# Attention, a mixture layer and a routed mixture in one kernel: the decoding of the weight pieces moves up in the scheduler's priority

## The chip, the cores and the metric

One core of a Trainium2 chip. The metric is the device time of one execution in microseconds, as the median of several runs of the same program. Engines: TensorE (PE in the profile, PEld its weight loads), VectorE (DVE), ScalarE (ACT), GpSimd (POOL) and SyncE (SP), which issues nearly all DMAs here.

## The reference

Three layers follow one another on 4 x 576 tokens of 512 numbers:

```python
# attention: 4 batches, 8 heads, 576 tokens, head size 64, block-causal mask (blocks of 64)
scores = where(block_i >= block_j, q @ k.T / 8, -1e9)
x = softmax(scores) @ v                                  # to [2304, 512]
# first mixture: three matrices 512 x 768, element-wise maximum, then 768 x 512
x = maximum(maximum(x @ w1, x @ w2), x @ w3) @ w_out
# second mixture: tokens with x @ w_skip > 0 go to the best of 8 experts (512 -> 1024 -> 512)
out = x.copy()
out[do] = x[do] + gate * (relu(x[do] @ w1[e]) @ w2[e])
```

## The kernel before, in words

The 2304 tokens are cut into 9 chunks of 256 (`CH`). A chunk's attention is cut into half units, one head of one query tile of up to 128 tokens; chunk 0 and chunk 1 have 16 each. A half unit goes through four steps, each one loop pass later than the one ahead: `s_scores` (L252: score matmuls into `sc`, the negated maximum `nm` on VectorE at L268, the exponential `p` on ScalarE at L273), `s_norm` (L279: the sum's reciprocal `r`, L289, and on GpSimd in the first chunks the product `p*r`, L292), `s_trans` (L296: transposes `tp` on TensorE and the copy `pT`) and `s_pv` (L312: the products `pv` for two heads, then `x`, L325 and L326). For each pair of heads, `load` (L191) asks for keys and queries (`kq`), `load_v` for values (`vt`), and `prep` (L214) splits them into two parts each (`kh`, `kl`, `q`).

Matmul operands are kept as a high and a low part, and three products of parts stand for one product. The weights of the first mixture arrive as int64 pairs and have to be decoded before they are split. `wprep(k)` (L145) does this. For k from 0 to 17 it takes one piece of w1, w2 or w3: a DMA of 512 KB into `raw` (L149, a ring of 3), one pass on ScalarE (L138), four on VectorE (L139 to L142, into `dec`, a ring of 6), the high part on ScalarE (L163) and the low part on GpSimd (L164), into the tile `w`. For k from 18 to 23 it takes one piece of w_out in the same way (`rawo`, one buffer; `deco`; `wo_h`, `wo_l`), and then TensorE transposes it (`pswt`, L168), ScalarE copies that (`wt`, L170), and TensorE multiplies it by the routing weights (`psw`, L173), which gives the routing matrix `wp` (L174, L175). The tiles `wo_h` and `wo_l` take the memory of the rings `raw` and `dec`, so no w_out piece can be split before the last w piece has been decoded and split.

The first mixture's work on a chunk is a generator, `moe_steps` (L434): 18 steps `m_h` of 12 matmuls each (`ps_h`, L338; 6 column blocks times w1, w2, w3), in which chunk 0 also calls `wprep` for the w_out pieces from step 16 on; then `m_logits` (`ps_l`, L359), which needs all of `wp`; then `m_y` (`ps_y`, L375) and the routing. All chunks but the last share one pair of tiles for the hidden layer, so chunk 1 cannot write its own before chunk 0's `m_y` has read it.

The main loop (L510 to L541) goes over half units. In each pass it writes down the attention steps, two calls of `wprep` while pieces of w1 to w3 are left (so all 18 are written within nine passes, in chunk 0), and, once chunk 1 has begun, some steps of the mixture. This is not the order of execution. The framework's scheduler takes instructions by priority, which is the place in the program less an offset, and fixes one order for each engine and for SP's DMA issues; every engine then executes in that order. `pri` (L507) gives the four attention steps an offset of 1000; `load`, `load_v`, `prep`, `wprep` and the mixture have none.

After chunk 8's attention the mixture is finished, and the second mixture (`Moe2`, L563) runs in an order written by hand.

Of the kernel before, what the change touches and what calls it, by code (L numbers as in the profile page):

```python
# [48 lines left out]
def kernel(  # L49
# [36 lines left out]
    wr_sb = const.tile([P, ND, NG], F32, name="wr_sb")  # L86

    _moe1_phase(tc, nc, const, small, locals())


def _moe1_phase(tc, nc, const, small, g):
# [10 lines left out]
    with ExitStack() as st_y:  # L102
# [88 lines left out]
        def load(i):  # L191
            if i >= len(groups):
                return
            c, b, qlo, qhi, tiles, hp = groups[i]
            gd = gdat[i]
            gd["raw"] = kvp.tile([P, 4, CH], F32, tag="kq", name="kq", bufs=3)
            if b == 0:
                for r0 in (0, 64):
                    nc.sync.dma_start(out=gd["raw"][r0:r0 + 64, :, 0:qhi - qlo], in_=kq0[hp, 0:64, :, qlo:qhi])
                return  # L200
            nc.sync.dma_start(out=gd["raw"][:, :, 0:qhi - qlo], in_=kqT[b - 1, hp, :, :, qlo:qhi])

        def load_v(i):
            if i >= len(groups):
                return
            c, b, qlo, qhi, tiles, hp = groups[i]
            gd = gdat[i]
            nkt = (qhi + P - 1) // P
            gd["v"] = kvp.tile([P, 5, P], F32, tag="v", name="vt", bufs=2)
            nc.sync.dma_start(  # L210
                out=gd["v"][:, 0:nkt, :],
                in_=v[b, 0:nkt * P, hp * P:(hp + 1) * P].rearrange("(t p) d -> p t d", p=P))
# [66 lines left out]
        def s_norm(k):  # L279
            i, c, hp, q0, nq, nk, col, j, first = hus[k]  # L280
            h = hd[k]
            su = h["su"]
            r = sm.tile([P, 1], F32, tag="r", name="r")
            eng = nc.gpsimd if c < 3 or (c < 0 and k % 2) else nc.vector
            if h["parts"] == 2:
                eng.tensor_scalar(r[:nq], su[:nq, 0:1], su[:nq, 1:2], 1e-9, op0=ALU.add, op1=ALU.add)
            else:
                eng.tensor_scalar(r[:nq], su[:nq, 0:1], 1e-9, None, op0=ALU.add)
            nc.vector.reciprocal(r[:nq], r[:nq])  # L289
            pt = h["p"][:nq, 0:nk]  # L290
            if c < 4 or (c < 0 and k % 2 == 0):
                nc.gpsimd.tensor_tensor(pt, pt, r[:nq, 0:1].to_broadcast([nq, nk]), op=ALU.mult)  # L292
            else:
                nc.vector.tensor_scalar(pt, pt, r[:nq, 0:1], None, op0=ALU.mult)

        def s_trans(k):  # L296
            i, c, hp, q0, nq, nk, col, j, first = hus[k]
            h = hd[k]
            nkt = (nk + P - 1) // P
            pT = pp.tile([P, 5, P], F32, tag="pT", name="pT")  # L300
            h["pT"] = pT
            for t0 in range(0, nkt, 4):
                n = min(4, nkt - t0)
                tp = ps_t.tile([P, 4, P], F32, tag="tp", name="tp")
                for t in range(n):
                    nc.tensor.transpose(tp[:, t, 0:nq], h["p"][:nq, (t0 + t) * P:(t0 + t + 1) * P], ident[:nq, :nq])  # L306
                if (k + t0) % 2 or c < 2:
                    nc.scalar.copy(pT[:, t0:t0 + n, 0:nq], tp[:, 0:n, 0:nq])  # L308
                else:
                    nc.vector.tensor_copy(pT[:, t0:t0 + n, 0:nq], tp[:, 0:n, 0:nq])  # L310
# [186 lines left out]
        wk = 0  # L497
# [9 lines left out]
        def pri(c):  # L507
            return tc.high_priority(1000 if c >= 0 else 0)

        for k in range(n_hu + 3):  # L510
            if k < n_hu:
                i, c, hp, q0, nq, nk, col, j, first = hus[k]
                if first:
                    load(i + 2)
                    load_v(i + 1)
                with pri(c):
                    s_scores(k)
                if first:
                    prep(i + 1)
            if 0 <= k - 1 < n_hu:  # L520
                with pri(hus[k - 1][1]):
                    s_norm(k - 1)
            if 0 <= k - 2 < n_hu:
                with pri(hus[k - 2][1]):
                    s_trans(k - 2)
            if 0 <= k - 3 < n_hu and hus[k - 3][7] == 1:
                with pri(hus[k - 3][1]):
                    s_pv(k - 3)
                if k - 3 + 1 == n_hu or hus[k - 2][1] != hus[k - 3][1]:
                    queue.append(moe_steps(hus[k - 3][1]))  # L530
            for _ in range(2):
                if wk < 18:
                    wprep(wk)
                    wk += 1
            if k == 0:
                constants()
            if k < n_hu and c > 0:
                credit += NM / per_chunk[c] * (0.8 if c == 1 else 1)
                while credit >= 1:
                    credit -= 1  # L540
                    run_moe()  # L541
# [301 lines left out]
```

## Time and profile before

| What | us |
|---|---|
| median of 3 runs | 765.43 |
| lowest and highest | 764.71, 770.18 |
| the profiled execution, own time | 770.52 |
| its span in the trace | 768.7 |

The profile is of one execution, the one of 770.52 us, of which the span covers 768.7. "Busy" is the time in which an engine executes; the idle time ahead of a group of instructions is given with the engine, tile and line that ended it. Matmuls overlap in the pipeline, so a single matmul's duration is longer than the distance to the next. `xN` is a count. Names of tiles are those of the program, with the numbers left out.

### The profile page before, as it was taken

To read this page: it belongs to the slowest core of one execution; us is meant where nothing else is said; L and a number is where in the kernel's file an instruction comes from. 1 tells how busy PE (TensorE), PEld (TensorE's weight loads), DVE (VectorE), ACT (ScalarE), POOL (GpSimd) and SP (SyncE) were. 2 spreads that over 40 slices of the span, in tenths; PEclk is the share of its full clock that TensorE was granted. 3 is DMA by queue.
4 is the path that set the end of the run, shared out by engine and by line. 5 is a ranking of instruction groups with operands and counts; after the bars stand their busy time and mean duration, and the time that the engine had idled before them with its cause. 6 is when DMAs were issued, how large, how long until landed. Compare 5 with 4: busy or idle time off the path is not lost. (4 is left out here: it accounts for less than half of the span.)

```text
span 768.7 us, 13867 instructions
## 1 busy us (share of the span) xinstructions
PE 668.7 (87%) x4774; PEld 569.6 (74%) x4774; DVE 492.7 (64%) x1291; ACT 375.7 (49%) x977; POOL 348.8 (45%) x434
## 2 busy tenths in 40 slices
PE   2667887889999999999999999999999764888775
PEld 1445776667997998988988978988989643666664
DVE  5898998854655765676765557666645404556774
ACT  4575656634544454545544445554436114354561
POOL 4777876753543322321111233211117608567783
PEclk9988999559999999999999999999999985998999
DMA  8963513433122124323102143212017938847730
GB/s 198 210 189 108 156 49 103 126 103 108 44 55 85 45 63 131 87 63 97 40 23 91 32 117 108 76 35 73 19 56 275 328 115 294 295 119 262 259 123 30
DMA packets 84861, 92.02 MB, mean 120 GB/s; under 512 B 11252, under 2 KB 61556, under 8 KB 84768
## 3 DMA queue, kind: packets, MB, share of 16 engines
q1 hardware_dynamic: 81104, 85.42, 36.9%
q0 software_dynamic: 2624, 5.45, 2.2%
q8 instruction: 47, 0.77, 0.4%
q14 instruction: 46, 0.38, 0.1%
q10 hardware_dynamic: 1040, 0.01, 0.1%
HBM read 80.17 MB, written 11.96 MB: 120 GB/s over the span
## 5 line engine op out<-in xcount | busy, mean ns | idle before, releaser
L338 PE MATMUL ps_h<-x,w 128*128 128x256 f32 x1944 | 275.4, 290 | 6.7 <-DVE x L326 2.4
L338 PEld LDWEIGHTS ps_h<-x,w 128*128 128x128 f32 x1944 | 251.5, 193 | 13.1 <-DVE x L326 3.3
L273 ACT ACTIVATE p<-sc,nm 64x288 f32<-64x288 f32 (+9 forms) x192 | 95.5, 500 | 51.2 <-PE tp L306 26.6
L306 PE MATMUL tp<-cst_sb,p 128*128 128x128 f32 (+1 forms) x480 | 90.9, 285 | 13.6 <-ACT pT L308 7.4
L268 DVE TENSOR_REDUCE nm<-sc 64x1 f32<-64x288 f32 (+9 forms) x192 | 84.9, 450 | 27.3 <-PE sc L263 24.1
L261 PE MATMUL sc<-kh,q 128*64 128x288 f32 (+9 forms) x192 | 71.8, 378 | 24.7 <-ACT p L273 14.3
L646 POOL TENSOR_TENSOR lo<-raw,hi 128x1024 fp32r<-128x1024 f32 x30 | 83.7, 2812 | 17.3 <-ACTq L774 9.6
L242 POOL TENSOR_TENSOR kl<-kq,kh 64x512 fp32r<-64x512 f32 (+3 forms) x48 | 52.3, 1089 | 83.3 <-ACT kh L241 82.8
L350 POOL TENSOR_TENSOR h_l<-hm,h_h 128x256 fp32r<-128x256 f32 x54 | 43.9, 814 | 94.5 <-ACT h_h L349 92.0
L306 PEld LDWEIGHTS tp<-cst_sb,p 128*128 128x128 f32 (+1 forms) x480 | 57.3, 147 | 32.4 <-issue 14.0
L323 PE MATMUL pv<-pT,vt 128*64 128x128 f32 (+1 forms) x960 | 75.6, 286 | 5.3 <-ACT pT L308 3.3
L646 DVE TENSOR_TENSOR lo<-raw,hi 128x1024 fp32r<-128x1024 f32 x30 | 66.6, 2231 | 17.1 <-ACT hi L642 14.9
L642 ACT CAST hi<-raw 128x2048 fp32r<-128x2048 f32 x30 | 56.4, 1904 | 29.3 <-PEq L774 17.7
L323 PEld LDWEIGHTS pv<-pT,vt 128*64 128x64 f32 x960 | 52.9, 147 | 22.4 <-issue 7.5
L292 POOL TENSOR_TENSOR p<-p,r 128x128 f32<-128x128 f32 (+8 forms) x72 | 57.4, 801 | 25.2 <-DVE r L289 20.1
L261 PEld LDWEIGHTS sc<-kh,q 128*128 128x128 f32 (+1 forms) x192 | 36.8, 193 | 37.6 <-ACT p L273 20.0
L263 PE MATMUL sc<-kl,q 128*64 128x288 f32 (+9 forms) x192 | 63.6, 336 | 0.5 <-DVE kl L182 0.5
L308 ACT COPY pT<-tp 128x256 f32<-128x256 f32 (+4 forms) x112 | 44.9, 401 | 37.2 <-PE tp L306 32.4
L277 POOL MEMSET p<- 128x64 f32 (+1 forms) x96 | 14.4, 156 | 99.0 <-PE tp L306 89.0
L310 DVE COPY pT<-tp 128x256 f32<-128x256 f32 (+4 forms) x80 | 35.1, 446 | 36.7 <-PE tp L306 36.2
L241 ACT CAST kh<-kq 128x512 fp32r<-128x512 f32 (+3 forms) x48 | 24.5, 511 | 49.1 <-DMA kq<-in_kqT_dram 43.1
L326 DVE TENSOR_TENSOR x<-pv,x 128x128 fp32r<-128x128 f32 (+1 forms) x80 | 21.6, 270 | 37.5 <-ACT x L325 37.3
(137 smaller groups left out, 1162.2 us busy)
## 6 DMA issues: line engine op xcount, KB each, us to landing
raw<-in_m_w_dram SPq DMA_DIRECT2D x32, 1024.0 KB
raw<-in_w_dram SPq DMA_DIRECT2D x18, 512.0 KB
kq<-in_kqT_dram SPq DMA_DIRECT2D x16, 512.0 KB
vt<-in_v_dram SPq DMA_DIRECT2D x16, 320.0 KB
x<-y SPq DMA_DIRECT2D x18, 256.0 KB
out_dram<-y SPq DMA_DIRECT2D x18, 256.0 KB
kq<-in_kq_dram SPq DMA_DIRECT2D x16, 256.0 KB
rawo<-in_w_out_dram SPq DMA_DIRECT2D x6, 512.0 KB
```

Source lines behind the costliest of these rows:

```text
L242: nc.gpsimd.tensor_tensor(kl[0:64, :, qlo:qhi], kraw[0:64], kh[0:64, :, qlo:qhi], op=ALU.subtract)
L261: nc.tensor.matmul(ps[:nq, 0:hi - lo], gd["q1"][:, j, q0:q0 + nq], gd["kh"][:, j, lo:hi], start=True, stop=False)
L263: nc.tensor.matmul(ps[:nq, 0:hi - lo], gd["q2"][:, j, q0:q0 + nq], gd["kl"][:, j, lo:hi], start=False, stop=True)
L268: nc.vector.tensor_reduce(nm[:nq, n:n + 1], pss[n][:nq, 0:hi - lo], axis=AX.X, op=ALU.max, negate=True)
L273: nc.scalar.activation(pt[:nq, lo:hi], pss[n][:nq, 0:hi - lo], AF.Exp, bias=nm[:nq, 0:1], accum_out=su[:nq, n:n + 1])
L292: nc.gpsimd.tensor_tensor(pt, pt, r[:nq, 0:1].to_broadcast([nq, nk]), op=ALU.mult)
L306: nc.tensor.transpose(tp[:, t, 0:nq], h["p"][:nq, (t0 + t) * P:(t0 + t + 1) * P], ident[:nq, :nq])
L308: nc.scalar.copy(pT[:, t0:t0 + n, 0:nq], tp[:, 0:n, 0:nq])
L323: nc.tensor.matmul(pv[64 * jj:64 * jj + 64, 0:nq], vt[:, t, 64 * jj:64 * jj + 64], hd[k - 1 + jj]["pT"][:, t, 0:nq], start=(t == 0), stop= ...
L338: nc.tensor.matmul(ps, a[:, d, :], x[:, d, :], start=(n == 0), stop=(n == 3 * ND - 1))
L642: self.nc.scalar.copy(self.w(e, s)[0], self.raw_of(4 * e + s))
L646: eng.tensor_tensor(lo[:, r], self.raw_of(4 * e + s)[:, r], hi[:, r], op=ALU.subtract)
```

## The change

The two calls of `wprep` in the main loop get the same offset as the attention steps.

```diff
@@ -530,7 +530,8 @@
             for _ in range(2):
                 if wk < 18:
-                    wprep(wk)
+                    with tc.high_priority(1000):
+                        wprep(wk)
                     wk += 1
```

The work is the same: each engine has as many instructions of each line as before (ScalarE has one table load listed at another line). The w_out pieces keep their priority. Lines below L533 have a number higher by one in the changed kernel. Three places show what the scheduler makes of it.

SP at the start, first before, then after. `raw` from in_w1, in_w2 and in_w3 are the first pieces of w1 to w3, `kq` from in_kq0 keys and queries of batch 0, and `vt` values.

```order
L199 DMA kq_120<-in_kq0_dram 64x4x256 x2
L472 DMA aux_sb_117<-in_aux_dram 64x576
L224 DMA auxk_125<-in_aux_dram 64x576
L210 DMA vt_139<-in_v_dram 128x2x128
L475 DMA cst_sb_65<-in_cst_dram 128x282
L199 DMA kq_142<-in_kq0_dram 64x4x256 x2
L210 DMA vt_148<-in_v_dram 128x2x128
L199 DMA kq_145<-in_kq0_dram 64x4x256 x2
L149 DMA raw_118<-in_w1_dram 128x4x256
L149 DMA raw_118<-in_w2_dram 128x4x256
```

```order
L149 DMA raw_118<-in_w1_dram 128x4x256
L149 DMA raw_118<-in_w2_dram 128x4x256
L149 DMA raw_118<-in_w3_dram 128x4x256
L199 DMA kq_120<-in_kq0_dram 64x4x256 x2
L472 DMA aux_sb_117<-in_aux_dram 64x576
L224 DMA auxk_125<-in_aux_dram 64x576
L210 DMA vt_139<-in_v_dram 128x2x128
L475 DMA cst_sb_65<-in_cst_dram 128x282
L199 DMA kq_142<-in_kq0_dram 64x4x256 x2
L149 DMA raw_118<-in_w1_dram 128x4x256
```

The first three w pieces now stand ahead of the first keys and queries, and the fourth ahead of the third pair of heads.

VectorE at the fifth w_out piece (`deco`), in chunk 2's attention, first before, then after; `q` belongs to the second pair of heads of batch 1.

```order
L141 SCALAR_TENSOR_TENSOR deco<-rawo,deco 128x512
L289 RECIPROCAL r<-r 64x1
L270 TENSOR_TENSOR nm<-nm 64x1
L238 COPY q_162<-q_1925 64x2x192
L239 SCALAR_TENSOR_TENSOR q_1925<-kq,q_1925 64x2x192
L326 TENSOR_TENSOR x<-pv,x 128x64
L142 SCALAR_TENSOR_TENSOR deco<-rawo,deco 128x512
L268 TENSOR_REDUCE nm<-sc 64x1
```

```order
L141 SCALAR_TENSOR_TENSOR deco<-rawo,deco 128x512
L174 CAST wp<-psw 128x10
L289 RECIPROCAL r<-r 64x1
L310 COPY pT<-tp 128x4x64
L310 COPY pT<-tp 128x64
L142 SCALAR_TENSOR_TENSOR deco<-rawo,deco 128x512
L175 TENSOR_TENSOR wp<-psw,wp 128x10
L268 TENSOR_REDUCE nm<-sc 64x1 x2
L238 COPY q_162<-q_1925 64x2x192
L239 SCALAR_TENSOR_TENSOR q_1925<-kq,q_1925 64x2x192
```

The piece's last pass (L142) moved ahead of the pair of instructions that prepare `q`.

ScalarE at the sixth w_out piece, from its first pass (L138) to its high part (L163), first before, then after; `kh_124` and `kh_158` are keys of batch 1, each cast once its DMA has landed.

```order
L241 CAST kh_124<-kq 128x2x256
L170 COPY wt<-pswt 128x512
L273 ACTIVATE p,su<-sc,nm 64x64
L138 ACTIVATE deco<-rawo 128x512
L325 CAST x<-pv 128x64
L308 COPY pT<-tp 128x4x64
L241 CAST kh_158<-kq 128x2x256
L308 COPY pT<-tp 128x64
L273 ACTIVATE p,su<-sc,nm 128x192 x2
L163 CAST wo_h<-deco 128x512
```

```order
L138 ACTIVATE deco<-rawo 128x512
L241 CAST kh_124<-kq 128x2x256
L237 ACTIVATE q_2105<-kq 128x2x192
L273 ACTIVATE p,su<-sc,nm 64x64
L163 CAST wo_h<-deco 128x512
L325 CAST x<-pv 128x64
L170 COPY wt<-pswt 128x512
L308 COPY pT<-tp 128x4x64
L308 COPY pT<-tp 128x64
L273 ACTIVATE p,su<-sc,nm 128x192
L241 CAST kh_158<-kq 128x2x256
```

The piece's first pass now stands ahead of the cast of `kh_124`, and its high part and the two copies `pT` ahead of the cast of `kh_158`.

## Rows read from the trace of the kernel before

**Rows 1.** The head of the page, and its line of TensorE's granted clock in 40 equal slices (19.2 us each), in tenths of full speed.

```profile
span 768.7 us, 13867 instructions
...
PEclk9988999559999999999999999999999985998999
```

**Rows 2.** Busy time by stretch from 200 us on. Columns: stretch, its length, then busy us and instructions of PE, PEld, DVE, ACT and POOL, the granted clock, the busy share of the DMA engines, GB/s.

```profile
200.00:300.00 100.00, 100.00 (x801) 89.58 (x802) 61.52 (x202) 48.86 (x154) 35.57 (x67) 1.00 0.23 67
...
500.00:560.00 60.00, 60.00 (x508) 54.82 (x508) 39.63 (x132) 27.07 (x84) 8.72 (x24) 1.00 0.13 41
```

**Rows 3.** The same view of the front of the program, in stretches that end where the text says: the first scores' maximum, the last w piece's decode, the second w_out piece's decode, the first `ps_l`, and TensorE without gaps.

```profile
0.00:14.70 14.70, 2.12 (x6) 1.50 (x6) 6.50 (x14) 4.87 (x9) 5.53 (x11) 1.00 0.79 169
14.70:111.50 96.80, 72.04 (x421) 55.20 (x422) 91.17 (x172) 60.98 (x166) 73.23 (x87) 0.93 0.62 155
111.50:123.70 12.20, 9.08 (x82) 7.29 (x81) 9.17 (x23) 9.04 (x26) 9.26 (x15) 1.00 0.22 60
123.70:155.00 31.30, 24.70 (x174) 19.50 (x174) 27.06 (x67) 19.86 (x62) 22.01 (x31) 0.68 0.42 120
155.00:170.60 15.60, 11.97 (x85) 10.34 (x84) 8.26 (x27) 7.22 (x23) 9.76 (x22) 0.50 0.39 119
170.60:178.00 7.40, 7.40 (x35) 5.47 (x35) 2.19 (x8) 1.88 (x6) 1.15 (x4) 0.64 0.15 38
```

**Rows 4.** VectorE's groups of instructions, shapes apart, from 14.70 to 111.50 us: line, engine, operation, names, shapes, count, busy us, mean ns, idle before it and who ended that.

```profile
L141 DVE SCALAR_TENSOR_TENSOR dec<-raw,dec 128x512 int32<-128x512 int32 x18 | 19.8, 1100 | 0.0
...
L139 DVE TENSOR_SCALAR dec<-dec 128x512 f32<-128x512 f32 x18 | 14.3, 800 | 4.0 <-ACT dec L138 3.9
...
L268 DVE TENSOR_REDUCE nm<-sc 128x1 f32<-128x512 f32 x7 | 4.7, 676 | 0.1
...
L289 DVE RECIPROCAL r<-r 128x1 f32<-128x1 f32 x28 | 4.3, 152 | 0.1
L326 DVE TENSOR_TENSOR x<-pv,x 128x128 fp32r<-128x128 f32 x12 | 3.4, 280 | 0.1
...
L345 DVE TENSOR_TENSOR hm<-ps_h,hm 128x256 f32<-128x256 f32 x4 | 1.6, 410 | 0.0
```

**Rows 5.** The start, in order of time, all engines: start us, duration, engine, line, operation, tiles, count, idle before it and who ended that.

```profile
0.75 1.33 SPq L199 DMA_DIRECT2D kq<-in_kq_dram  x2
...
6.35 1.28 ACT L237 ACT_TABLE_LOAD   x1 [6.35 <-DMA kq<-in_kq_dram]
...
8.30 0.42 DVE L238 CAST q<-q 64x512 fp32r<-64x512 f32 x1 [6.62 <-ACT q L237]
...
11.83 1.15 SPq L149 DMA_DIRECT2D raw<-in_w_dram  x2
...
13.58 0.51 SPq L149 DMA_DIRECT2D raw<-in_w_dram  x1
...
14.70 0.80 DVE L268 TENSOR_REDUCE nm<-sc 128x1 f32<-128x128 f32 x3
...
18.05 0.67 ACT L138 ACTIVATE dec<-raw 128x512 f32<-128x512 f32 x1 [0.74 <-DMA raw<-in_w_dram]
...
23.72 0.67 ACT L138 ACTIVATE dec<-raw 128x512 f32<-128x512 f32 x1 [2.14 <-DMA raw<-in_w_dram]
```

**Rows 6.** The decoded tile `dec`, 0 to 120 us: count, min/median/max ns, first and last start.

```profile
L139 DVE TENSOR_SCALAR dec<-dec x18: 404/548/1483, 19.4 to 105.8; 128x512 f32<-128x512 f32 x18
L140 DVE TENSOR_SCALAR dec<-dec x18: 402/420/1454, 20.9 to 107.5; 128x512 int32<-128x512 int32 x18
L141 DVE SCALAR_TENSOR_TENSOR dec<-raw,dec x18: 666/1016/2193, 21.6 to 108.6; 128x512 int32<-128x512 int32 x18
L142 DVE SCALAR_TENSOR_TENSOR dec<-raw,dec x18: 665/682/1556, 24.8 to 110.8; 128x512 int32<-128x512 int32 x18
```

**Rows 7.** The w_out pieces: SP's DMA issues, then VectorE, then ScalarE, then TensorE, each in order of time.

```profile
155.01 0.47 SPq L160 DMA_DIRECT2D rawo<-in_w_out_dram  x1
...
150.90 0.67 DVE L141 SCALAR_TENSOR_TENSOR deco<-rawo,deco 128x512 int32<-128x512 int32 x1
...
154.30 0.68 DVE L142 SCALAR_TENSOR_TENSOR deco<-rawo,deco 128x512 int32<-128x512 int32 x1
...
162.34 0.69 DVE L142 SCALAR_TENSOR_TENSOR deco<-rawo,deco 128x512 int32<-128x512 int32 x1
...
159.90 0.67 ACT L138 ACTIVATE deco<-rawo 128x512 f32<-128x512 f32 x1
...
163.96 0.62 ACT L241 CAST kh<-kq 128x512 fp32r<-128x512 f32 x1 [3.02 <-DMA kq<-in_kqT_dram]
...
166.01 1.12 PE L168 MATMUL pswt<-cst_sb,deco 128*128 128x128 f32 x4
...
170.60 0.38 PE L359 MATMUL ps_l<-h_h,wp 128*20 128x256 f32 x1
```

**Rows 8.** TensorE at the full clock, chunk 2's attention.

```profile
124.70 0.60 PE L306 MATMUL tp<-cst_sb,p 128*128 128x128 f32 x4
...
128.35 0.29 PE L261 MATMUL sc<-kh,q 128*64 128x288 f32 x1
128.48 0.29 PE L263 MATMUL sc<-kl,q 128*64 128x288 f32 x1
129.23 1.09 PE L323 MATMUL pv<-pT,vt 128*64 128x128 f32 x16 [0.46 <-DVE pT L310]
```

## Prediction

> **What bounds the kernel now.** I read the granted clock by slices first, then busy time by stretch, then VectorE's groups, then the order of time at the two places that the change touches. From 200 us to 560 us TensorE is busy without a gap at the full clock [rows 1, 2]. The two kernels run the same work there, so there the change can gain nothing directly. What it can change is how early TensorE gets there. In the front VectorE is the busy one: from the first maximum of scores (14.70 us) to the end of the last w piece's decoding (111.50 us) it executes 91.17 of 96.80 us, while TensorE executes 72.04; in the next 12.20 us it executes 9.17 [rows 3]. After that no engine is full: from 123.70 to 170.60 us the six w_out pieces follow one another, one at a time through a single raw buffer, and TensorE, partly at 0.50 of its clock, waits among attention's steps for the sixth of them before the first `ps_l` at 170.60 [rows 3, 7]. From there TensorE has no gap [rows 3].
>
> So the time is: when does the first `ps_l` start, and how much of TensorE's work is still to do then. I counted both programs' orders. On TensorE they have executed the same instructions of every kind by the end of the seventh `ps_y` tile (115 score pairs, 262 transposes, 258 `pv`, 864 `ps_h`) and by each later one, so nothing behind that point adds a term.
>
> **The change, part by part.** Nothing is added or removed. Four things move.
>
> *The decoding ends earlier, but the orders meet again.* In the new order VectorE finishes the eighteenth w piece with 26 maxima, 23 reciprocals, 9 evictions of `x` and 4 of the mixture behind it, where it had 30, 28, 12 and 8. At 0.676, 0.152, 0.280 and 0.410 us each [rows 4] that is 2.7 + 0.8 + 0.8 + 1.6 = 5.9 us less work, so the last w piece would be done some 6 us sooner. It buys little: in both orders GpSimd's low part of the second w_out piece stands behind exactly the same work (13 key splits, 32 sums, 33 products, 18 w pieces, 5 of the hidden layer), and VectorE's decoding of it behind nearly the same (35 maxima against 34, 32 reciprocals and 14 evictions in both). What is taken from attention ahead of the last w piece is paid between it and the second w_out piece. Only idle time can differ at that meeting place, which was at 123.70 us.
>
> *The start.* The first `raw` takes the place of the first `kq`: 512 KB each, issued at 0.75; the keys let ScalarE start at 6.35 and VectorE at 8.30 [rows 5]. I take the same for the first piece, so VectorE starts work when it did, with decoding. Three pieces then stand ahead of the first maximum. At the shortest durations that the trace has for the four passes (0.404, 0.402, 0.666 and 0.665 us [rows 6]) they take 3 x 2.14 = 6.4 us, so the first maximum comes at 14.7 + 6.4 = 21.1 us. VectorE was busy in those 6.4 us before and is busy after: cost nothing, as long as VectorE's work is the pace. If that cover is gone, it costs the 6.4 us.
>
> *Idle time up to the meeting place.* Before, VectorE idled 96.80 - 91.17 = 5.63 us in the long stretch, 4.0 of them ahead of L139, waiting for raw data by way of ScalarE [rows 3, 4], and 12.20 - 9.17 = 3.03 us behind it. After, the stretch behind the last w piece holds 5.9 us more of VectorE's work, 15.1 us. At the idle share of that stretch (3.03 in 12.20, a quarter) it idles 5.0 us there, 2.0 more. The stretch ahead is shorter and asks for raw data sooner, for which I give back 1.0 of the 4.0. Sum +1.0. The bounds are -8.7 (all 8.66 us of idle time go) and +6.4 on top of +1.0 (attention's late start is kept whole).
>
> A rule speaks to this. L141 has a least time of 0.666, a median of 1.016 and a most of 2.193 us for one shape [rows 6]. The Trainium skill's SBUF — State Buffer, "Who interferes with whom", says that a VectorE instruction with two SBUF inputs and a GpSimd instruction that reads SBUF exclude each other for their whole length; the spread agrees. By that rule the three first pieces, decoded while GpSimd has little to do, would save 3 x (1.100 - 0.666) = 1.3 us, and the sum below would be 762.4. I leave this out, because the twelve later splits still meet VectorE's passes.
>
> *The fifth and sixth w_out piece.* L141 of the fifth ended at 151.57 and its L142 began at 154.30, behind the `q` pair; at 155.01 SP issued the sixth [rows 7]. In the new order four small instructions stand between; by the distance of such rows about 0.7 us, so 2 us are saved. The sixth piece's L142 ended at 163.03, but its transposes began at 166.01, because the `pv` ahead of them on TensorE waited for a `pT` copy, which waited on ScalarE behind the cast of a key tile whose DMA landed at 163.96 [rows 7]. That cast now stands behind the copies: up to 3.0 us more. Against that, the cast of the other key tile now stands between the piece's first pass and the later copies; I take off 0.5. Together -4.5; bounds 0 (another wait takes over, most likely keys' DMAs) and -5.7 (2.73 + 2.98).
>
> *What is left at the first `ps_l`.* There the new order has executed 53 score pairs, 120 transposes and 110 `pv` instead of 55, 124 and 120. At the full clock the distances are 0.26 us for a pair, 0.15 and 0.068 [rows 8]: 0.5 + 0.6 + 0.7 = +1.8 us, to be done in TensorE's full stretch. This is a count, and sure.
>
> Sum: +1.0 - 4.5 + 1.8 = -1.7 us. The profiled execution took 770.52 us, which would become 768.8. It is 5.1 us over the median of the runs shown; on the median the sum gives 765.43 - 1.7 = 763.7 us.
>
> **The rivals.** A measurement of this kernel can tell about 1% from no change, 7.65 us: faster is below 757.8, slower above 773.1.
>
> *Slower: attention is late and stays late.* Place: the chain from a maximum over exponential, reciprocal, product, transpose, copy and `pv`, in chunk 1, once the decoding no longer fills VectorE. Price: the 6.4 us of the start, the +1.0, no gain at the w_out pieces, since keys and queries then come later too, and the 1.8: +9.2, 774.6 us. It decides from the point at which VectorE idles more than about 15 us up to the meeting place instead of 8.7. For it: VectorE already idled a quarter of the time right after the last w piece [rows 3], and the raw pieces asked for at 11.83 and 13.58 landed at 18.05 and 23.72, so what stands behind others lands 6 to 10 us late [rows 5]. Against it: in the long stretch VectorE had 94% of its time filled, with attention's steps ready. The Trainium skill's DMA: Bandwidth & Descriptors, "Queues, rings and completion order", says that an engine's DMAs use one ring on each DMA engine and are taken up in ring order. By that rule the first keys stand behind 1.57 MB; at the 169 GB/s of the first stretch [rows 3] they land 9.3 us later, at 15.6, and the first maximum would come some 2 us later still, which makes this rival 776.6 us. The landing times in those rows agree with it, and it is why I give this rival more than one in ten.
>
> *Faster: the idle time goes.* With weights ready sooner, TensorE's mixture steps no longer wait and half of the 8.7 us of VectorE's idle time goes, and the w_out pieces gain the whole 5.7: -4.3 - 5.7 + 1.8 = -8.2, 757.2 us. For it: 4.0 us of that idle time are waits for raw data. Against it: a ring of 3 raw tiles still asks for a piece only when the one three before is decoded.
>
> *Faster: the clock.* From 155 us to the first `ps_l` TensorE ran at 0.50 of the full clock, and at 0.64 on the mean until 178.00 [rows 3], after a stretch in which it was busy about four fifths of the time. If the new order keeps it busier there, 11.97 x 0.50 + 7.40 x 0.36 = 8.7 us of its work go: -1.7 - 8.7 = -10.4, 755.0 us. Nothing in the order says that it will be busier, and the opposite would lengthen the spell.
>
> **How the numbers follow.** Forecast, 763.7 us with its own range from 757.9 to 773.0: 0.61. Late attention, 774.6: 0.19. Idle time gone, 757.2: 0.12. Clock, 755.0: 0.08. Hence faster 0.20, within 1% 0.61, slower 0.19. The range goes from 755.0, the clock rival, to 775.0, just past late attention, and leaves out no more than two in ten.
>
> **What would show it.** In the changed kernel's profile: VectorE's first passes are L139 to L142 and begin between 8 and 9 us; the first maximum comes at 20 to 23 us; the last L142 of a w piece ends at 104 to 108 us; the second w_out piece's L142 ends within 3 us of 123.7; the first `ps_l` starts at 165 to 169 us, and TensorE has no gap from there. The forecast is wrong if the second w_out piece is more than 6 us off 123.7 either way, if the sixth piece's transposes still begin behind a key cast on ScalarE, or if a difference arises behind the seventh `ps_y` tile, where the orders are the same.

## The result, and the profile of the changed kernel

The changed kernel is slower: 776.36 us (median of 7 runs) against 768.64 us (7 runs), ratio 1.0122 with a 95% interval of 1.0082 to 1.0161. The forecast was 763.7 us, the range 755.0 to 775.0; the rival that comes nearest is late attention, 774.6 us. A second set of runs of the same two programs gave 1.0103 [1.0047, 1.0160]. Each was profiled twice, and the marks of the two profiles are (us):

| mark | before | changed | mean difference |
|---|---|---|---|
| first maximum (L268) starts | 14.70, 14.58 | 21.89, 21.56 | +7.1 |
| chunk 0's last `x` copy (L325) | 67.57, 65.17 | 82.24, 81.14 | +15.3 |
| L142 of the second w_out piece starts | 122.13, 119.28 | 127.31, 127.53 | +6.7 |
| first `ps_l` | 170.60, 168.09 | 171.86, 171.64 | +2.4 |
| sixth `y` copy (L378) | 300.34, 297.44 | 303.21, 303.59 | +4.5 |
| seventh `y` copy | 347.15, 345.50 | 352.85, 356.75 | +8.5 |
| eighteenth and last `y` copy | 626.96, 623.39 | 631.21, 635.35 | +8.1 |
| end of the span | 768.7, 763.5 | 777.5, 778.7 | +12.0 |

The loss has arisen by the seventh `y` copy. What is added in the second mixture is not settled: from its first gather into `xg` (L654, L655 in the changed kernel) to the end it took 132.7 and 131.1 us before, 137.4 and 134.5 after, but 130.4 in `first3` below, whose ratio is as high as the changed kernel's.

The changed kernel's start, its columns as in [rows 5]: SP, ScalarE, then VectorE.

```profile
0.74 1.53 SPq L149 DMA_DIRECT2D raw<-in_w_dram  x3
2.32 1.39 SPq L199 DMA_DIRECT2D kq<-in_kq_dram  x2
...
0.75 1.28 ACT L138 ACT_TABLE_LOAD   x1 [0.75 <-PEq L831]
4.57 0.66 ACT L138 ACTIVATE dec<-raw 128x512 f32<-128x512 f32 x1 [2.53 <-DMA raw<-in_w_dram]
12.09 0.63 ACT L237 ACTIVATE q<-kq 128x512 fp32r<-128x512 f32 x1 [1.21 <-DMA kq<-in_kq_dram]
...
5.26 0.43 DVE L139 TENSOR_SCALAR dec<-dec 128x512 f32<-128x512 f32 x1 [3.58 <-ACT dec L138]
21.89 0.28 DVE L268 TENSOR_REDUCE nm<-sc 128x1 f32<-128x128 f32 x1
```

The keys were asked for 1.6 us later than in [rows 5], behind three transfers of 0.5 MB, and ScalarE could use them at 12.09 us, 5.7 us after the 6.35 at which it waited no longer for them before. VectorE began at 5.26, earlier than the 8 to 9 of the forecast: ScalarE could use the first piece at 4.57 us, not at 6.35, and its table load, which stood behind the keys' arrival before, was over by then. The Trainium skill's DMA: Bandwidth & Descriptors, "Queues, rings and completion order", from which I had worked out 15.6 us as an estimate, says that each ring is consumed in order; the 12.09 us agree in direction. The rate that I gave it, 169 GB/s, was too low: the DMA engines moved 226 GB/s in the first 12.09 us.

The stretches of [rows 3] in the changed kernel, same columns.

```profile
0.00:14.70 14.70, 0.00 (x0) 0.00 (x0) 7.29 (x12) 6.35 (x12) 4.46 (x11) 1.00 0.94 222
14.70:111.50 96.80, 64.48 (x361) 49.15 (x362) 90.45 (x169) 59.66 (x160) 73.06 (x87) 0.82 0.55 144
111.50:123.70 12.20, 12.20 (x104) 10.76 (x103) 4.84 (x15) 7.34 (x22) 5.96 (x11) 1.00 0.19 54
123.70:155.00 31.30, 25.34 (x181) 19.58 (x179) 23.29 (x62) 19.70 (x60) 20.03 (x28) 0.79 0.39 120
155.00:170.60 15.60, 12.83 (x90) 10.44 (x89) 12.41 (x33) 7.92 (x25) 9.69 (x15) 0.50 0.34 99
```

In the long stretch VectorE is as full as before (90.45 of 96.80 us), but TensorE executes 64.48 us instead of 72.04 (361 matmuls instead of 421), at a mean clock of 0.82 instead of 0.93. In the second profiles it is 363 matmuls instead of 436 with 0.91 in both, so the work is missing without a lower clock too. In the next stretch it is the other way round: TensorE has no gap, and VectorE executes 4.84 us instead of 9.17. I read this as the price of the order, since TensorE's work here comes from attention; the experiments below test it.

Where TensorE's bulk of chunk 0's mixture begins, ScalarE's last `x` copy of chunk 0 and TensorE, in the kernel before:

```profile
67.57 0.28 ACT L325 CAST x<-pv 128x128 fp32r<-128x128 f32 x1
...
71.69 1.70 PE L338 MATMUL ps_h<-x,w 128*128 128x256 f32 x12 [1.09 <-ACT ha L342]
```

and in the changed kernel:

```profile
82.24 0.26 ACT L325 CAST x<-pv 128x128 fp32r<-128x128 f32 x1
...
82.56 1.01 PE L338 MATMUL ps_h<-x,w 128*128 128x256 f32 x3 [0.32 <-ACT x L325]
...
89.54 1.69 PE L338 MATMUL ps_h<-x,w 128*128 128x256 f32 x12
```

Only three `ps_h` tiles can be open at a time, and none is complete before the last of chunk 0's `x`. The matmuls at 82.56 wait for it; the first group of 12 in a row stands at 89.54, 17.9 us later than before. The weights came earlier (the last w piece's L142 starts at 98.89 instead of 110.78), but they were not what came last. This lateness alone is not the price, though: in first1 below the last `x` comes at 75.23 us and the first such group (24 in a row) at 81.23, 9.5 us later than before, and no time is lost.

The end of the w_out pieces, as in [rows 7]:

```profile
127.31 0.69 DVE L142 SCALAR_TENSOR_TENSOR deco<-rawo,deco 128x512 int32<-128x512 int32 x1
...
166.85 1.38 DVE L142 SCALAR_TENSOR_TENSOR deco<-rawo,deco 128x512 int32<-128x512 int32 x1
...
168.28 1.12 PE L168 MATMUL pswt<-cst_sb,deco 128*128 128x128 f32 x4
...
171.86 0.38 PE L359 MATMUL ps_l<-h_h,wp 128*20 128x256 f32 x1
```

The sixth piece's transposes follow its decoding at once, as forecast; before they began 3.0 us behind it [rows 7].

And one gap that the forecast did not have, behind the sixth `y` copy. The changed kernel, in order of time (SP, ScalarE, TensorE):

```profile
307.94 1.79 SPq L201 DMA_DIRECT2D kq<-in_kqT_dram  x2
...
313.99 0.62 ACT L241 CAST kh<-kq 128x512 fp32r<-128x512 f32 x1 [3.33 <-DMA kq<-in_kqT_dram]
...
315.80 0.62 ACT L241 CAST kh<-kq 128x512 fp32r<-128x512 f32 x1 [0.76 <-DMA kq<-in_kqT_dram]
...
316.63 0.26 ACT L308 COPY pT<-tp 128x128 f32<-128x128 f32 x1
...
316.94 1.31 PE L323 MATMUL pv<-pT,vt 128*64 128x128 f32 x20 [2.37 <-ACT pT L308]
```

The same place in the kernel before (SP, ScalarE):

```profile
305.26 0.55 SPq L201 DMA_DIRECT2D kq<-in_kqT_dram  x1
...
309.65 0.62 ACT L241 CAST kh<-kq 128x512 fp32r<-128x512 f32 x1 [2.75 <-DMA kq<-in_kqT_dram]
```

SP asks for two pairs of keys in a row, and both land late; both casts stand on ScalarE ahead of a `pT` copy, and TensorE waits 2.37 us for that. Before, one pair was asked for here; TensorE had no gap in this profile and one of 1.16 us in the second, in which that cast waited 4.44 us. In the second profile of the changed kernel the first cast waited 4.59 us and TensorE 3.5 us, and TensorE's granted clock was 0.50 from 317 to 322 us.

### The profile page after: what moved, and what is told of

It is laid out like the page before. It is cut to its first block, busy times and chain, and to the rows that moved or that the text cites. A ratio compares the mean times of both kernels' runs of the same rounds, so it can differ in the third digit from the quotient of the medians.

```text
span 777.5 us, 13867 instructions
## 1 busy us (share of the span) xinstructions
PE 670.9 (86%) x4774; PEld 571.1 (73%) x4774; DVE 491.7 (63%) x1291; ACT 377.8 (49%) x977; POOL 345.3 (44%) x434
## 5 line engine op out<-in xcount | busy, mean ns | idle before, releaser
L268 DVE TENSOR_REDUCE nm<-sc 64x1 f32<-64x288 f32 (+9 forms) x192 | 85.0, 450 | 40.0 <-PE sc L263 36.8
L306 PE MATMUL tp<-cst_sb,p 128*128 128x128 f32 (+1 forms) x480 | 93.8, 287 | 14.0 <-POOL p L292 8.0
L323 PE MATMUL pv<-pT,vt 128*64 128x128 f32 (+1 forms) x960 | 79.2, 286 | 5.3 <-ACT pT L308 4.0
L647 DVE TENSOR_TENSOR lo<-raw,hi 128x1024 fp32r<-128x1024 f32 x30 | 69.2, 2318 | 15.9 <-ACT hi L643 15.3
L294 DVE TENSOR_SCALAR p<-p,r 128x576 f32<-128x576 f32 (+9 forms) x88 | 41.4, 472 | 4.3
```

The lines of the kernel that those rows point to most:

```text
L268: nc.vector.tensor_reduce(nm[:nq, n:n + 1], pss[n][:nq, 0:hi - lo], axis=AX.X, op=ALU.max, negate=True)
L323: nc.tensor.matmul(pv[64 * jj:64 * jj + 64, 0:nq], vt[:, t, 64 * jj:64 * jj + 64], hd[k - 1 + jj]["pT"][:, t, 0:nq], start=(t == 0), stop= ...
L647: eng.tensor_tensor(lo[:, r], self.raw_of(4 * e + s)[:, r], hi[:, r], op=ALU.subtract)
```

## The experiments

Ratios are to the kernel before on the same chip, with 95% intervals. "Keys" is the start of ScalarE's first pass on the first keys and queries (L237); where the table load waits for the keys (first maximum before 15 us, and late_keys), it lies 1.28 us behind their arrival. "Maxima" is the number of maxima (L268) that VectorE has started when the last pass on the last w piece starts: the fewer, the earlier the decoding stands. "Idle" is TensorE's idle time in the first 181 us of the profile; it depends on the granted clock too, which was 0.77 to 0.89 there. All columns but the ratio are of one profiled execution, and those lie up to 5 us off the median of their kernel.

| kernel | keys | first maximum | maxima | chunk 0's last `x` | idle | ratio |
|---|---|---|---|---|---|---|
| before | 7.64 | 14.70 | 30 | 67.57 | 50.7 | 1 |
| changed | 12.09 | 21.89 | 26 | 82.24 | 55.7 | 1.0122 [1.0082, 1.0161] |
| same_again | 11.72 | 21.56 | 26 | 81.14 | 55.2 | 1.0103 [1.0047, 1.0160] |
| first3 | 10.85 | 20.57 | 27 | 79.25 | 58.8 | 1.0114 [1.0068, 1.0160] |
| late_keys | 12.81 | 19.87 | 30 | 78.72 | 57.6 | 1.0089 [1.0049, 1.0129] |
| gap_prep3only | 10.75 | 20.51 | 26 | 80.94 | 54.7 | 1.0073 [1.0044, 1.0102] |
| raws_pool | 8.71 | 19.13 | 28 | 75.60 | 55.9 | 1.0029 [1.0009, 1.0049] |
| first1 | 7.80 | 15.93 | 27 | 75.23 | 46.9 | 0.9989 [0.9963, 1.0016] |
| from3 | 7.53 | 14.57 | 29 | 78.64 | 55.2 | 1.0034 [0.9998, 1.0071] |
| start_first | 7.55 | 14.60 | 30 | 71.40 | 53.5 | 1.0029 [0.9992, 1.0067] |
| att0 | 7.62 | 14.67 | 29 | 70.01 | 44.9 | 1.0026 [0.9994, 1.0058] |
| b_loads | 7.67 | 14.73 | 29 | 69.89 | 48.6 | 1.0042 [1.0014, 1.0071] |
| b_wokq | 7.53 | 14.58 | 30 | 65.95 | 46.0 | 1.0022 [0.9996, 1.0048] |
| before_light | 7.59 | 14.64 | 34 | 67.76 | 52.4 | 1.0029 [1.0001, 1.0058] |
| after_light | 11.32 | 21.12 | 28 | 81.92 | 63.2 | 1.0109 [1.0075, 1.0142] |
| before_again | 7.53 | 14.58 | 30 | 65.17 | 51.4 | one execution |

The theory after the result was that the late start is the cost; the rivals were the later pieces' place in the order, the transfers' bunching, the gap, and scatter.

**same_again**, the changed kernel once more.

> The changed kernel unaltered, for a second profile of it and more times. In its first profile the last first-mixture output copies stand 4.2 to 5.8 us behind those of the kernel before, and the span 8.8, so some 4.6 us come to the difference inside the second mixture, whose order is the same in both. Theory A (all of the loss that is the change's own arises before the second mixture: late attention, two half units more left over, and a key transfer waited for at 315 us): the 4.6 us are scatter between executions, and the profile of this one has the first gather of the second mixture 4 to 6 us later than before's 636.0, a second mixture within 3 us of before's 132.7 us (first gather to end) or at least other than 137.4. Theory C (the second mixture is slower after the change, by its clock or its transfers): again 137 us or more from the first gather to the end. The ratio to the kernel before is 1.008 to 1.016 under both.

First gather at 644.2 us, 8.2 later than before's, so more than the 4 to 6 expected, and 134.5 us from there to the end. That is theory A's side; theory C's 137 us do not repeat.

**first3** and **from3** take the change apart.

```diff
-                    with tc.high_priority(1000):
+                    with tc.high_priority(1000 if wk < 3 else 0):    # first3
+                    with tc.high_priority(1000 if wk >= 3 else 0):   # from3
```

> Only the first three pieces get the offset, so only SP's start and the engines' heads change: three raw transfers ahead of the first keys, VectorE's decoding ahead of the first maximum. It leaves four tp tiles fewer behind the first ps_l than the changed kernel (57 half units have their tp ahead of it, against 53; before: 55). Theory A1 (the loss comes from the start: the keys behind 1.5 MB of raws, first maximum at 21.9 us instead of 14.7, TensorE short of work up to 80 us): first maximum at 21 to 23 us, first ps_l at 174 to 176 us, later than in the changed kernel since it stands behind four more half units, and the time 771 to 778, ratio 1.006 to 1.014. Theory A2 (the loss comes from the later pieces' place ahead of chunk 1's attention): ratio 0.996 to 1.003.

> The offset for all pieces but the first three: the start is that of the kernel before (keys first, first maximum at 14 to 15 us), and behind it the order is the changed kernel's (53 half units ahead of the first ps_l, as there). Theory A1 (the loss comes from the start): first maximum 14 to 15 us, last w piece's last pass done at 104 to 109 us, first ps_l at 168 to 170 us, and the time within 3 us of the kernel before, ratio 0.996 to 1.004. Theory A2 (the loss comes from the later pieces): ratio 1.008 to 1.016, as the whole change.

The first three pieces alone cost as much as all eighteen. Their first `ps_l` came at 177.5 us, later than the 174 to 176 expected; behind the sixth `y` copy there is no gap (44.9 us to the seventh), so nothing of this loss comes from there. The fifteen others cost 0.3%, not told from nothing. But they hardly moved: 29 maxima stand ahead of the last w piece, 30 before and 26 in the changed kernel, and that piece's last pass began at 110.86 us, where it was to be done at 104 to 109. So from3 says little on the later pieces' place. Its first `ps_l` came at 172.4 us, not at 168 to 170, and the gap behind the sixth `y` copy is there (2.4 us).

**start_first** keeps all eighteen and puts the first loads back in front.

```diff
+        with tc.high_priority(5000):
             load(0)   # ... to load(1), the code ahead of the loop
```

> The change, with the loads and the splitting of the first half units (the code in front of the loop) raised by 5000, so that SP asks for three pairs' keys, values and constants ahead of the first raw transfer; all 18 pieces keep their offset. 56 half units stand ahead of the first ps_l (before 55). Theory A1 (the raws ahead of the first keys cost the time): first maximum at 12 to 15 us and a time of 764 to 771, ratio 0.995 to 1.003. Theory A2 (the pieces' place ahead of the later attention costs it): ratio 1.006 to 1.016.

As the theory has it. But the decoding fell back together with the start: 30 maxima stand ahead of the last w piece, as before, so this run does not part the late start from the early decoding. **first1** and **raws_pool** are doses between.

```diff
+                    with tc.high_priority(1000 if wk < 1 else 0):    # first1
-                nc.sync.dma_start(
+                (nc.gpsimd if k < 3 else nc.sync).dma_start(         # raws_pool, in the changed kernel
```

> Only the first piece gets the offset: one raw transfer of 0.5 MB ahead of the first keys, one piece decoded ahead of the first maximum (three in first3, none in the kernel before). 55 half units stand ahead of the first ps_l, as in the kernel before. Theory A1 (each piece in front of attention delays it by 2.3 to 2.5 us, and TensorE, which is the pace from 90 us on, does not make that up): first maximum at 16.5 to 18 us, first pswt 2 to 3 us behind the 114.2 of before, ratio 1.000 to 1.006, a third of first3's. Theory A3 (a threshold: a start that is late by less than VectorE's slack costs nothing): first pswt within 1 us of 114.2 and ratio 0.996 to 1.001.

> The change, but GpSimd's queue issues the first three raw transfers, so on SP's the first keys, values and constants stand in front again; VectorE's order then has one piece's decoding ahead of the first maximum, and 57 half units are ahead of the first ps_l. Theory Q (the ring's order is the cost: keys behind 1.5 MB): first maximum at 15 to 19 us and a ratio of 0.997 to 1.005. Theory O (the raws cost the keys the same time from whatever queue, since the 16 engines share them): first maximum at 20 to 23 us and ratio 1.007 to 1.015.

One piece ahead costs nothing that can be measured, though the first `pswt` came at 116.6 us instead of 114.2 (A1's mark, A3's ratio). Its keys are usable almost as early as before, while the last w piece stands behind 27 maxima, as in first3, and chunk 0's last `x` comes 7.7 us later than before. So decoding that early, without late keys, lost nothing. In raws_pool SP asks for the keys at 0.74 us and GpSimd for the three raws from 1.31 on; ScalarE takes the keys at 8.71 us, straight behind a decoding pass that had waited for its raw until 8.15. The first maximum comes at 19.13, just outside theory Q's 15 to 19, and most of the loss is gone.

**late_keys** tests the step itself: the kernel before, keys late, nothing decoded earlier.

```diff
+        with tc.high_priority(6000):
+            for i in range(3):
+                nc.sync.dma_start(out=dec_t[:, 2 * i:2 * i + 2]..., in_=ws[i][:, 0:2 * P]...)
         load(0)
```

> The kernel before, without the change, with three extra transfers of 0.5 MB (the first raws, copied a second time into the memory of dec, whose contents nobody reads) ahead of the first keys on SP: attention starts late and nothing is decoded in that time. 57 half units stand ahead of the first ps_l, as in first3. The step of the prediction under test is that a late start of attention costs nothing as long as VectorE's work is the pace. Theory K (the start by itself is the cost): first maximum at 19 to 22 us, chunk 0's last x copy at 73 to 82 us, TensorE idle in the first 181 us 54 to 60 us, ratio 1.006 to 1.014. Theory P (the start costs nothing by itself; the decoding passes in front of the half units do): first maximum 19 to 22 us, ratio 0.998 to 1.004.

Theory K. The first maximum is 5.2 us late, and 0.9% is lost, with as many maxima ahead of the last w piece as before. ScalarE at the keys:

```profile
11.52 1.28 ACT L237 ACT_TABLE_LOAD   x1 [11.52 <-DMA kq<-in_kq_dram]
```

Two things differ besides the start: 1.5 MB more are moved, and the scheduler fixed another order behind it (57 half units ahead of the first `ps_l` instead of 55). Busy time in the first 181 us, columns as in [rows 2]; in the kernel before, then in late_keys, then in att0 (next):

```profile
0.00:181.00 181.00, 130.30 (x814) 101.06 (x815) 145.15 (x310) 105.26 (x295) 122.69 (x170) 0.85 0.53 135
```

```profile
0.00:181.00 181.00, 123.44 (x786) 98.61 (x788) 144.24 (x308) 102.61 (x292) 120.13 (x169) 0.88 0.54 143
```

```profile
0.00:181.00 181.00, 136.13 (x803) 106.70 (x804) 141.45 (x311) 103.22 (x286) 118.78 (x160) 0.82 0.50 134
```

VectorE executes the same in before and late_keys (145.15 and 144.24 us), TensorE 6.9 us less (786 matmuls instead of 814, at a clock of 0.88 instead of 0.85). In the changed kernel the row reads:

```profile
0.00:181.00 181.00, 125.25 (x792) 98.01 (x792) 140.03 (x298) 103.53 (x284) 116.79 (x160) 0.81 0.49 132
```

**att0** leaves the change in and moves only chunk 0's attention ahead of it again, with its loads and its splitting.

```diff
-            return tc.high_priority(1000 if c >= 0 else 0)
+            return tc.high_priority(3000 if c == 0 else 1000)   # chunk 0's load, load_v and prep at 3000, the code ahead of the loop at 5000
```

> The change stays (all 18 pieces at the offset 1000), but chunk 0's attention with its loads and splitting stands at 3000, so ahead of the decoding again. Theory X (what is lost is chunk 0's last attention output: it is finished at 82.2 us in the changed kernel and at 67.6 in the kernel before, and the bulk of chunk 0's mixture, TensorE's work, waits for it and not for the weights): first maximum at 14 to 16 us, chunk 0's last x copy at 64 to 72 us, TensorE idle in the first 181 us 47 to 54 us (before 50.7, changed 55.7), ratio 0.995 to 1.004; it has the two key requests in a row behind the sixth output copy, which takes 2 to 3 us of that. Rival R (the early decoding costs by itself, since its transfers and passes come in one bunch): x at 64 to 72 us all the same, but a ratio of 1.007 to 1.014.

Theory X's ratio, and its last `x` at 70.0 us; idle is below the 47 to 54 expected, and of the gap expected behind the sixth `y` copy 0.6 us came. The decoding keeps its offset but not its place (29 maxima), so att0, like start_first, gives the start back and the early decoding up together.

**before_light** and **after_light** ask why a late start costs.

```diff
+                np_ = 1 if c == 0 else 3
-                    for a, x in (...three products...):
+                    for a, x in (...three products...)[:np_]:    # and the stop flag with it
```

> The kernel before, in which chunk 0's first mixture leaves out two of its three products of parts (TensorE has 144 matmuls less there, some 15 us by the distances in its busy stretches); the partner of after_light. First ps_l at 162 to 170 us and a time of 756 to 768.

> The changed kernel with the same products of chunk 0 left out, so that TensorE is no longer full between 90 and 131 us. Theory T (the late attention costs because TensorE is the pace once the decoding is over): the loss goes, since VectorE's work, which is the same in both, then sets the pace: the sixth output copy stands no later than 1 us behind that of before_light, and the time is within 3 us of before_light's or below it. Theory V (TensorE is not what holds it; what follows the decoding is a chain through VectorE, GpSimd and the single rawo buffer that is late by itself): the first pswt in after_light is again 5 to 8 us behind that of before_light's, and the time 6 to 10 us above before_light's.

before_light 1.0029 [1.0001, 1.0058], after_light 1.0109 [1.0075, 1.0142]: about 0.8% between the two, not told from the 1.0 to 1.2% without the cut. Theory T's time is not met. Its mark at the sixth `y` copy is met in name only: after_light has it at 293.04 us, before_light at 295.02, but with 6 score pairs, 13 transposes and 20 matmuls of `pv` fewer behind it, an estimate of 4 to 5 us by the distances in [rows 8]. So a TensorE that is full from 90 to 131 us looks like a consequence of the late attention and not like what makes it cost. The test is not clean, because the granted clock up to 181 us fell with the matmuls (0.80 and 0.77, without the cut 0.85 and 0.81); 144 matmuls fewer in chunk 0 gave the kernel before nothing, 773.39 us where I expected 756 to 768. Theory V's marks are not met either: the first `pswt` is 4.0 us later (107.84 against 103.83), the time 5.0 us longer.

**gap_prep3only** takes the two key requests behind the sixth `y` copy apart.

```diff
-                    prep(i + 1)
+                    with tc.high_priority(200 if 3 <= c <= 3 else 0):
+                        prep(i + 1)
```

> The changed kernel, with the splitting of chunk 3's keys (prep) raised by 200. Up to some 130 us the order is the changed kernel's; behind that 55 half units instead of 53 stand ahead of the first ps_l, and SP no longer asks for two pairs of keys in a row between the sixth and the seventh ps_y. Theory G (of the loss, 2.4 to 3.5 us is TensorE's gap at 315 us, where ScalarE waits for those two transfers in front of a pT copy): no gap of TensorE over 1 us between the sixth and the seventh output copy, 44 to 47.5 us from the one to the other (49.6 and 53.2 in the changed kernel's two profiles), ratio 1.003 to 1.009. Rival (the gap is made up elsewhere): ratio 1.010 to 1.014.

No such gap, and 45.7 us from the sixth to the seventh copy; ratio 1.0073, as theory G has it, though its interval overlaps with the change's, and 55 half units instead of 53 stand ahead of the first `ps_l`.

**b_loads** and **b_wokq** try the other direction, on the kernel before.

```diff
+                    with pri(c):        # b_loads: load, load_v, and prep alike; the code ahead of the loop at 5000
+                        load(i + 2)
-                raw = apool.tile([P, 4 * P, 2], I32, name="rawo")    # b_wokq
+                raw = kvp.tile([P, 4 * P, 2], I32, tag="kq", name="rawo", bufs=3) if k % 2 else apool.tile(...)
```

> The kernel before, without the change, with the loads and the splitting of all half units at the attention's offset of 1000: attention is moved ahead of the decoding even further, the opposite of the change. Theory X: chunk 0's last x copy at 60 to 68 us, TensorE idle in the first 181 us 46 to 51 us, ratio 0.993 to 1.002 (two key requests in a row behind the sixth output copy here too). Rival R (the weights' decoding was already late in the kernel before, and is later now): the eighteenth piece's low part later than 118 us and a ratio of 1.002 to 1.010.

> The kernel before, with every second w_out piece read into the ring of the keys (kq) instead of the single rawo buffer, so that the request of the next piece need not wait for the decoding of the last: does the chain of six w_out pieces (8 to 10 us each, 114 to 166 us) hold the first ps_l, whatever comes before? Theory W (the single buffer holds it): 7 to 9 us from pswt to pswt in the mean instead of 10.4, first ps_l at 162 to 168 us, ratio 0.993 to 1.000. Rival (attention's place in the engines' orders holds it): still 10 us from pswt to pswt, ratio 0.998 to 1.006.

Neither helps. b_loads' last `x` is no earlier (69.89 us), and its weights are no later (the last w piece's low part starts at 111.4 us, before at 112.7), so both theories miss their place; its 0.4% lie in R's range. TensorE waits 2.4 us for ScalarE's `p` behind 181 us. In b_wokq a w_out piece takes 9.6 us in the mean instead of 10.4, more than theory W's 7 to 9; the first `ps_l` comes at 165.2 us, and the time is the same. So the second buffer hardly shortens the chain, and a first `ps_l` that is 3 to 5 us earlier was not worth a time that can be measured.

**before_again**, the kernel before once more.

> The kernel before unaltered, for a second profile. All theories: chunk 0's last x copy at 66 to 69 us, first ps_l at 169 to 172 us, TensorE idle in the first 181 us 49 to 52 us and no gap behind the sixth output copy. Open is the second mixture: from the last output copy of the first mixture to the end 139 to 146 us.

First `ps_l` at 168.1 us and last `x` at 65.2, each almost 1 us below what I gave, and a gap of 1.16 us behind the sixth `y` copy, where I expected none. In front of that copy the two executions of this one program differ by up to 2.9 us. From the last `y` copy to the end it took 140.1 us.

Read together, the ratio goes with the keys. Where ScalarE has them by 7.8 us, no kernel is more than 0.42% behind the kernel before; raws_pool, at 8.71, loses 0.3%; the six with 10.75 to 12.81 lose 0.7 to 1.2%. It does not go with the place of the decoding (27 maxima and no loss in first1, 30 and 0.9% in late_keys) nor with chunk 0's last `x` (75.23 us in first1, 78.64 in from3). On the marks, from3's profiled execution is not typical: it took 777.93 us, 3.8 more than the median of its runs.

No version tried beats the kernel before by what can be measured.

## Why the prediction was wrong, point by point

**The step that failed is "The start": "VectorE was busy in those 6.4 us before and is busy after: cost nothing, as long as VectorE's work is the pace."** The time of the first maximum came out (21.89 us, 21.1 worked out), in part by luck: I had the keys in time and the decoding in front of them. In fact VectorE began 3.0 us earlier than I took it to, waited 2.25 us for the third piece, and the keys came 5.7 us late; in late_keys, with nothing decoded ahead, the first maximum still comes at 19.87. The cost, nothing, did not come out. late_keys shows that the late start costs by itself, 0.9% with VectorE as busy as before and the decoding no earlier; first1 shows that decoding which is nearly as early by the last w piece costs nothing when the keys are in time; in start_first and att0 the loss goes when the start is given back, though the decoding falls back with it. So VectorE's work was not interchangeable: my reading, argued and not shown, is that maxima let TensorE go on, and decoding does so only where a weight comes last. My evidence, 94% of VectorE's time filled in the long stretch, showed a full engine and not that its order was free.

**"Idle time up to the meeting place", +1.0.** Measured +6.7 at the second w_out piece (mean of two profiles each): close to the upper bound that I gave, +7.4. Up to the end of that piece's decoding (128.00 us) VectorE idled 14.05 us in the changed kernel:

```profile
14.70:128.00 113.30, 80.98 (x496) 63.71 (x496) 99.25 (x195) 69.41 (x188) 82.04 (x101) 0.85 0.50 132
```

against 8.66 before, near the 15 from which the rival was to decide. The term that was mis-sized is the idle time behind the last w piece:

```profile
100.37:128.00 27.63, 27.63 (x227) 24.07 (x225) 14.25 (x42) 16.47 (x46) 18.96 (x29) 1.00 0.15 42
```

VectorE executes 14.25 us there (15.1 worked out) but idles 13.4, not 5.0: I carried over the idle share of a stretch in which TensorE had gaps, and here TensorE has none. The last w piece itself was done 11.1 us sooner, not 6: VectorE had executed 5.4 us less by then (5.9 worked out) and idled 5.7 us less. My mark for a failure, more than 6 us off 123.7, was too wide to show it (128.0).

**"The fifth and sixth w_out piece", -4.5.** Right: from the second piece's L142 to the first `ps_l` it took 44.3 us instead of 48.6 in the means of the two profiles, -4.3, and the sixth piece's transposes no longer begin behind a key cast.

**"What is left", +1.8.** The count holds, one price does not: [rows 8] has 16 matmuls of `pv` in 1.09 us, so 0.068 for one, and a `pv` of the count is two of them. The ten are 1.4 us and not 0.7, and the term is +2.5. From the first `ps_l` to the sixth `y` copy the difference grows from 2.4 to 4.5 us, by 2.1, with two score pairs and two transposes still open there.

**"Nothing behind that point adds a term."** Behind the seventh `ps_y` tile this held (+8.5, then +8.1 at the eighteenth copy). But I counted instructions at the marks and did not read SP's order between them: from the sixth to the seventh copy the two orders differ, and 4.0 us arise there in the mean. TensorE's wait for the key transfers is 2.4 and 3.5 us there, 0 and 1.2 before, so 2.3 of the 4.0.

So the sum was -1.7 and should have been -1.7 + 5.7 (idle) + 4.0 (from the sixth to the seventh copy) = +8.0; the medians differ by 7.7. That closes the sum for this kernel and proves no single term: first3 and late_keys have no such gap (44.9 us from the sixth to the seventh copy), stand 7 us behind at the sixth copy already, and lose about as much.

**The rivals.** Late attention was right that the start stays late and that VectorE idles behind the last w piece; its chain within chunk 1 was not tested by itself. That its 774.6 us comes nearest is in part luck: its sum counted no gain at the w_out pieces (-4.3 came) and missed the sixth to the seventh copy (+4.0), and the two cancel. "Idle time gone" named what fell away (L139's wait for data), but TensorE's mixture steps did not wait for weights; they waited for `x`. The clock rival did not come: 0.50 from 155 us on as before, and in the long stretch no higher than before in either pair of profiles (0.82 against 0.93, 0.91 against 0.91).

What stays open: by which waits keys that are 3 to 5 us late become 7 to 9 us of the whole time, and why 5 to 7 us at the first maximum become 12 to 15 at chunk 0's last `x`; why raws_pool, with its first maximum and its idle sum near late_keys', loses only 0.3%, so that neither number alone tells the time; whether the 1.5 MB more or the other order has a share in late_keys' loss; and the second mixture's scatter.

## What to carry to other kernels

An engine that is full is not proof that the order of its work is free: ask of each piece of it who waits, and leave in front what everything else starts with, here the first keys and queries and not the weights. Raising the priority of work that begins with a large transfer raises the transfer too, in front of the small one that everything starts with; keep the first loads ahead of it. A count of instructions at marks says that the work is equal there, not that the order between them is; read the DMA queue's order up to the point where both orders are the same.

## What the runs showed of the hardware

A request of 512 KB on SP's queue, behind the sixth `y` copy, was usable 4.4 and 5.7 us after its issue in the two profiles of the kernel before (305.26 to 309.65, 302.77 to 308.44); with a second one asked for right behind it the first took 6.1 and 6.2 us in those of the changed kernel (307.94 to 313.99, 308.49 to 314.70). That is little beyond the scatter. In the profile in which TensorE then had a gap of 3.5 us, its granted clock stood at the lower level (0.50) from 317 to 322 us; in the other, with a gap of 2.4 us, it stayed at 1.00. With three transfers of 0.5 MB ahead of the keys on SP's queue ScalarE used the keys from 10.85 to 12.81 us on (first3, late_keys and the changed kernel); with the three on GpSimd's queue, asked for 0.6 us behind the keys, at 8.71; without them at 7.53 to 7.67.
